# Second halves of six early loads issued from ScalarE's queue

## The chip, the core and the metric

The kernel runs on one core of one Trainium2 chip. A core has five engines that run side by side: TensorE (matmuls, PE in the profile, with its weight loads as PEld), VectorE (DVE), ScalarE (ACT), GpSimd (POOL) and SyncE (SP), which here only issues DMAs. The metric is the device time of one execution in microseconds (us); the less the better.

## The reference

Two layers follow each other, for 8 batches of 576 tokens. The first is a linear attention with 8 heads of 64, normalised per head; the second is a mixture of 4 attention experts, of which each token uses two. In short:

```python
kv  = einsum('bhsd,bhse->bhde', k, v)
out = einsum('bhsd,bhde->bhse', q, kv)
x   = out / sqrt(mean(out * out, -1) + 1e-6) * g_norm        # then heads side by side: [b, 576, 512]
logits = x @ w_gate                                          # top 2 of 4 experts, softmax over the two
for e in range(4):
    a = softmax(causal(x @ wq[e] @ (x @ wk[e]).T / 8))
    y += gate[e] * (a @ (x @ wv[e]) @ wo[e])
```

Inputs are q, k and v of shape (8, 8, 576, 64) and the weights, all float32.

## The kernel before

The work is cut by batch, and within a batch into five blocks of tokens, four of 128 and one of 64. For each batch `kv` (line 405) makes the 64x64 products of k and v for four pairs of heads; k and v come in large loads `lk` and `lv` of the first 512 tokens (line 306) and in two small ones each, `lkr` and `lvr`, of the last 64 tokens (line 322), one for each half of the heads. The product is copied to the tile `kvx` (`kvc`, lines 283 and 285), multiplied with the gate weights (`kgm`, line 425), summed (`kgr`, line 432), and the sums are put beside it (`kgx`). `out` (line 466) then multiplies a block of transposed q with it. For batches 0 and 1 q is transposed by matmuls with an identity (`q`, line 448) from blocks that `lq` loads (line 336), each block by two DMAs, one for each half of the heads; from batch 2 on VectorE transposes it (line 456). Then come the norm, the transposition of the normalised tokens (`x`, line 567), the projections to v (line 626), q and k (line 645) of the experts, attention (lines 672, 686, 706), the output product (line 764) and the stores. The weights of the experts are loaded early into `w_stage` (`lw`, line 378) and scaled by g_norm (`ws`, line 384).

Nothing is scheduled by the compiler: `ORDER` is one long list of tasks written out by hand, and each engine, and each DMA queue, executes its own tasks in that order. `ENGINE` says for copies and elementwise tasks which engine does them, and `SLOTS` which buffer a tile takes. Loads and stores are issued by SyncE, except in batch 0 for the loads of v, which ScalarE issues at the very start (`queue`, line 290). Around the change the list reads, in order (task, batch, part; the engine for those of ScalarE):

```
lvr 0 (ACT), lq 0,4, lv 0,0 (ACT), lk 0,2, lv 0,1 (ACT), lkr 0, lv 0,2 (ACT), lv 0,3 (ACT), lk 0,1, q 0,4, lk 0,3,
gb, qc 0,4 (ACT), lk 0,0, lq 1,2, lq 0,3, kv 0,2, lq 0,0, gr, g8, lvr 1, kv 0,1, wg, kv 0,3, lq 0,2, kv 0,0,
kgm 0,1, kvc 0,1, lq 0,1, kvc 0,0 (ACT), kgm 0,0, kgr, lk 1,1, q 0,3, lq 1,4, kgx, lv 1,0, out 0,4, lkr 1, lk 1,0, lv 1,1, lw v,1 ...
```

In batch 0 a `lk` or `lv` brings two heads (256 KB), later four (512 KB). A half of a q block of 128 tokens is 128 KB, a half of a remainder 64 KB. `ZEROS` puts filler matmuls on zeros ahead of some tasks of the start (line 796).

Of the kernel before, what the change touches and what calls it, by code (L numbers as in the profile page):

```python
# [16 lines left out]
NB, NCH, EP, NF = 5, 4, 2, 4  # L17
# [5 lines left out]


ZEROS = {("q", 0, 4): 8, ("gb",): 2, ("kv", 0, 2): 6, ("kv", 0, 1): 3, ("q", 0, 3): 3}

ORDER = (
    "090E010403080507020u060H0v003F0D0c0A0F0G3C0b0J0I0d0C0a0j0i0B0e0f0k390s0g3H0l0m0h0t381A0n163B1C1B1D0w3718170o19"
# [90 lines left out]
def kernel(  # L119
# [13 lines left out]
    nc = tc.nc  # L133
    P = nc.NUM_PARTITIONS
    B, H, S, Dh = q.shape
# [3 lines left out]
    REM = S - NF * P  # L139
# [72 lines left out]
    kr, vr, kvx, lg8s, vexts, mss, sqs, rstds, roots = [], [], [], [], [], [], [], [], []  # L212
# [77 lines left out]
    def queue(b, second):  # L290
        return nc.scalar if b == 0 and second else nc.sync

    def q_t(b):
        if b in QPE:
            return buf(("q", b), [P, NB, 2, NCH * Dh], FP32, "q_b")
        return buf(("q", b), [P, NCH, S // 32, 32], FP32, "q_b")
# [19 lines left out]
        if (b, p) == (0, NCH - 1):  # L316
            nc.scalar.preload_act_table_set("natural_log_exp_and_others")

    def load_rem(eng, dst, src, b):
        for a in range(2):  # L320
            hs = slice(a * NCH, (a + 1) * NCH)
            eng.dma_start(dst[a * REM : (a + 1) * REM, hs, :], src[b, hs, NF * P : S, :].rearrange("h p d -> p h d"))

    def lkr(b):
        load_rem(nc.sync, kr[b % 2], k, b)

    def lvr(b):
        load_rem(queue(b, True), vr[b % 2], v, b)

    def lq(b, i):  # L330
        eng = nc.sync
        if b in QPE:
            t0, nt = blocks[i]
            n = NCH * nt // P * Dh
            for a in range(2):
                eng.dma_start(
                    q_t(b)[:, i, a, 0:n], q[b, a * NCH : (a + 1) * NCH, t0 : t0 + nt, :].rearrange("h (p j) d -> p h (j d)", p=32)
                )
            return
        r, c0, n = i % 4, i // 4 * 2, 2 * (S // 32)  # L340
        h0 = NCH * (r // 2) + c0
        eng.dma_start(
            q_t(b)[r * 32 : (r + 1) * 32, c0 : c0 + 2].rearrange("p c g d -> p (c g) d"),
            q[b, h0 : h0 + 2, :, (r % 2) * 32 : (r % 2 + 1) * 32].rearrange("h (g t) d -> t (h g) d", t=32),
        )
# [427 lines left out]
    def store(b, qc):  # L773
# [4 lines left out]

    emit = dict(
        lk=lk, lv=lv, lkr=lkr, lvr=lvr, lq=lq, gr=gr, g8=g8, gb=gb, wg=wg, lw=lw, ws=ws, lwo=lwo, wo=wo,  # L780
        kv=kv, kvc=kv_copy, q=q_tr, qc=q_copy, kgm=kvg_mul, kgr=kvg_sum, kgx=kvg_copy,
        out=out_mm, oc=o_copy, sq=square, red=red, ln=ln, rs=rs, na=newton_a, nb=newton_b, nc=newton_c, nd=newton_d, gl=gl, lg=lg, xm=xm, x=x_tr, xc=x_copy,
# [5 lines left out]
    def zero_matmuls(n, count):  # L788
        if n[0] == "kv":
            t, lo = small("kv", n[1]), NCH * Dh  # L790
        elif n[0] in ("q", "x", "v", "y"):
            t, lo = small(*n), 0
        else:
            t, lo = big(*{"qp": ("q",), "kp": ("k",)}.get(n[0], (n[0],)), *n[1:])[:, 0], 0
        for _ in range(count):
            nc.tensor.matmul(
                t[:, lo:512], lhsT=zeros[:, 0:P], rhs=zeros[:, lo:512], start=True, stop=True, skip_group_check=True
            )
# [28 lines left out]
    with tc.manual_schedule():  # L827
        for n in order:
            touched.clear()
            traced = len(nc.cur_bb.bb.instructions)  # L830
            if n in ZEROS:
                zero_matmuls(n, ZEROS[n])
            emit[n[0]](*n[1:])
# [32 lines left out]
```

The softmax here doesn't subtract the row's maximum and nothing guards it: scores larger than these inputs give would overflow.

## Time and profile before

| | before |
|---|---|
| time, median of 3 runs | 226.26 us (225.9 to 227.05) |
| span of the profiled execution | 225.8 us |
| TensorE busy | 211.3 us (94%) |
| VectorE busy | 157.5 us (70%) |
| ScalarE busy | 133.5 us (59%) |
| GpSimd busy | 125.8 us (56%) |
| moved by DMA | 40.29 MB, mean 178 GB/s |
| read from HBM, written to it | 30.42 MB, 9.44 MB |

A share of busy time is a mean over the span. In the first 60 us, where the loads of batches 0 to 3 and all weights arrive, the engines are less busy than later: TensorE works for 8.21 of the first 10 us and 8.41 of the next, and for all of the 20 us from 60 to 80. In the timelines that follow, a row gives the start, the length, the engine, the line, the operation, what it writes and reads, and how many are merged in the row; in square brackets stands the idle time of the engine just before, with what ended it. SPq and ACTq are the instructions by which SyncE and ScalarE issue DMAs; their length is the time of the issuing, not of the transfer.

### The profile page before, as it was taken

What the parts mean: (1) busy time and instruction counts of PE and PEld (TensorE: products, weight loads), DVE (VectorE), ACT (ScalarE), POOL (GpSimd) and SP (SyncE); (2) the same over time, 40 slices, a digit from 0 to 9 for tenths busy, and PEclk for the clock granted to TensorE, in tenths of its full rate; (3) what the DMA queues carried; (4) which work ended last, traced back from release to release, by engine and by line L of the source; (5) the groups of instructions that cost most, each with busy time, mean ns of one, the idle gap of its engine ahead of it and who ended that gap; (6) DMA issues with size and microseconds to landing.
All of it is one profiled execution on the core that took longest, in us unless ns stands there. A gap on an engine that the chain in (4) does not pass through costs nothing. (4 is left out here: it accounts for less than half of the span.)

```text
span 225.8 us, 6620 instructions
## 1 busy us (share of the span) xinstructions
PE 211.3 (94%) x2562; PEld 178.9 (79%) x2562; DVE 157.5 (70%) x366; ACT 133.5 (59%) x265; POOL 125.8 (56%) x278
## 2 busy tenths in 40 slices
PE   7988798988999998999999999999999999999981
PEld 3467797977899798897998699878878899799550
DVE  6275669738475798689797865589996476843570
ACT  0215742876649752759526964866764992664951
POOL 8400775077517693469715970479549869712520
PEclk9999999999699999999999999999999999999998
DMA  4988978998999677999899897998334000040065
GB/s 124 325 233 258 302 181 219 346 231 123 164 321 251 121 176 242 197 167 203 218 248 255 254 237 197 162 221 177 82 99 161 3 0 4 23 186 3 0 215 209
DMA packets 92576, 40.29 MB, mean 178 GB/s; under 512 B 66688, under 2 KB 88192, under 8 KB 92544
## 3 DMA queue, kind: packets, MB, share of 16 engines
q1 hardware_dynamic: 90784, 38.68, 71.2%
q10 hardware_dynamic: 1632, 1.18, 1.9%
q8 instruction: 20, 0.33, 0.7%
q14 instruction: 12, 0.10, 0.2%
q0 software_dynamic: 128, 0.01, 0.0%
HBM read 30.42 MB, written 9.44 MB: 177 GB/s over the span
## 5 line engine op out<-in xcount | busy, mean ns | idle before, releaser
L686 ACT ACTIVATE PT<-p 128x1024 bf16<-128x1024 f32 (+1 forms) x64 | 50.3, 841 | 6.6 <-PE p L672 6.1
L692 POOL TENSOR_SCALAR_AFFINE_SELECT PT<-PT 128x256 bf16<-128x256 bf16 (+1 forms) x80 | 29.1, 382 | 26.7 <-ACT PT L686 25.8
L557 POOL TENSOR_TENSOR x_tok<-o_sb,rstd 128x512 fp32r<-128x512 f32 x40 | 43.1, 1130 | 0.5
L466 PE MATMUL p<-kvx,qT 128*128 128x136 f32 (+1 forms) x320 | 39.1, 285 | 0.7 <-DVE kvx L285 0.7
L466 PEld LDWEIGHTS p<-kvx,qT 128*128 128x128 f32 (+1 forms) x320 | 34.7, 179 | 3.2 <-DVE kvx L285 0.9
L502 DVE TENSOR_REDUCE ms<-sq 128x8 f32<-128x520 f32 (+1 forms) x40 | 27.0, 684 | 7.5 <-POOL sq L498 3.6
L498 POOL TENSOR_TENSOR sq<-o_sb 128x512 f32<-128x512 f32 (+1 forms) x20 | 20.6, 1038 | 12.7 <-DVE ms L502 6.4
L626 PE MATMUL p<-wv_r,xT 128*128 128x256 f32 x160 | 25.9, 298 | 1.4 <-POOL wv_r L384 0.7
L567 PE MATMUL p<-ident_r,x_tok 128*128 128x128 f32 (+1 forms) x160 | 23.4, 279 | 0.7 <-DVE vext L285 0.3
L626 PEld LDWEIGHTS p<-wv_r,xT 128*128 128x128 f32 x160 | 21.5, 195 | 2.7 <-issue 0.8
L567 PEld LDWEIGHTS p<-ident_r,x_tok 128*128 128x128 f32 x160 | 20.6, 191 | 3.8 <-POOL x_tok L557 1.0
L672 PE MATMUL p<-qTp,kT 64*128 64x64 f32 (+4 forms) x192 | 22.2, 346 | 1.3 <-DVE kT L285 0.6
L283 ACT COPY o_sb<-p 128x544 f32<-128x544 f32 (+1 forms) x29 | 15.1, 532 | 13.0 <-PE p L466 12.6
L764 PE MATMUL p<-wo_b,OT 128*128 128x512 bf16 (+1 forms) x96 | 20.4, 348 | 0.7 <-ACT OT L283 0.5
L405 PE MATMUL p<-v_b,k_b 128*64 128x64 f32 x512 | 20.1, 224 | 0.9 <-DMA k_b<-in_k_dram 0.9
L645 PE MATMUL p<-xT,wk_r 128*128 128x288 f32 x128 | 20.8, 305 | 0.0
L405 PEld LDWEIGHTS p<-v_b,k_b 128*64 128x64 f32 x512 | 17.8, 138 | 3.2 <-issue 2.1
L645 PE MATMUL p<-xT,wq_r 128*128 128x288 f32 x128 | 19.8, 300 | 0.0
L672 PEld LDWEIGHTS p<-qTp,kT 64*128 64x128 f32 x192 | 14.4, 188 | 6.4 <-ACT PT L686 1.4
L645 PEld LDWEIGHTS p<-xT,wk_r 128*128 128x128 f32 x128 | 17.6, 188 | 1.5 <-DVE xT L285 0.5
L285 DVE COPY o_sb<-p 128x544 f32<-128x544 f32 (+1 forms) x19 | 12.0, 630 | 9.5 <-PE p L466 4.2
L706 PEld LDWEIGHTS <-PT 128*128 128x128 bf16 x480 | 16.2, 98 | 2.4 <-issue 0.8
(111 smaller groups left out, 348.2 us busy)
## 6 DMA issues: line engine op xcount, KB each, us to landing
out_dram<-y SPq DMA_DIRECT2D x32, 256.0 KB, 2.5
k_b<-in_k_dram SPq DMA_DIRECT2D x14, 512.0 KB, 6.4
v_b<-in_v_dram SPq DMA_DIRECT2D x14, 512.0 KB, 6.0
q_b<-in_q_dram SPq DMA_DIRECT2D x48, 144.0 KB, 4.7
q_b<-in_q_dram SPq DMA_DIRECT2D x16, 128.0 KB, 3.9
k_b<-in_k_dram SPq DMA_DIRECT2D x4, 256.0 KB, 5.4
v_b<-in_v_dram ACTq DMA_DIRECT2D x4, 256.0 KB, 5.2
k_rem<-in_k_dram SPq DMA_DIRECT2D x16, 64.0 KB, 5.1
```

Source lines behind the costliest of these rows:

```text
L405: nc.tensor.matmul(p_kv[hh * Dh : (hh + 1) * Dh, c, :], lhsT=lhs, rhs=rhs, start=(j == 0), stop=(j == NF), skip_group_check=True,)
L466: nc.tensor.matmul(p_o[p0 : p0 + nt, c // 2, c % 2 * 256 : c % 2 * 256 + 2 * GW], lhsT=qTs[b % NQT][:, c * S + i * P : c * S + i * P + nt] ...
L498: nc.gpsimd.tensor_tensor(out=dst, in0=src, in1=src, op=AluOpType.mult)
L502: nc.vector.tensor_reduce(mss[b % 2][:nt, i, :], sqs[(NB * b + i) % 3][:nt], axis=AX_X, op=AluOpType.add)
L557: nc.gpsimd.tensor_tensor(out=buf(("x", b, i), [P, NCH, P], FP32R, "x_tok")[:].rearrange("p c (h r) -> p h r c", h=H), in0=ob[:, i, :, 0:D ...
L567: nc.tensor.matmul(p_t[:, c * P : c * P + nt], lhsT=tiles["x", b, i][:, c, :], rhs=ident_r[:, 0:nt], start=True, stop=True)
L626: nc.tensor.matmul(p_v[:, 0 : E * Hd], lhsT=blocks_of(xTs[b % 2], c)[:, i * P : (i + 1) * P], rhs=w_r["v"][:, c, :, :].rearrange("p e f -> ...
L645: nc.tensor.matmul(p_p[:, s, 0:HALF], lhsT=w_r[nm][:, c, 2 * pr : 2 * pr + 2, :].rearrange("p e f -> p (e f)"), rhs=blocks_of(xTs[b % 2], ...
L672: nc.tensor.matmul(p_s[:, el, o : o + hi - lo], lhsT=kTs[(2 * b + pr) % 3][pp, kb * P : (kb + 1) * P], rhs=tiles["qTp", b, pr][pp, lo:hi], ...
L686: nc.scalar.activation(PT[:, :, d0 : d0 + o], big("sc", b, pr, j)[:, :, 0:o], ACTF.Exp, scale=scale)
L692: nc.gpsimd.affine_select(out=d, in_=d, compare_op=AluOpType.is_ge, fill=0.0, base=0, pattern=[[0, 2], [1, w]], channel_multiplier=-1,)
L764: nc.tensor.matmul(p_y[o * nq : (o + 1) * nq, 0:w], lhsT=lhs, rhs=wo_b[:, pr, o * w : (o + 1) * w], start=(pr == 0), stop=(pr == EP - 1), ...
```

## The change

Six loads of the start, each made of two DMAs for the two halves of the heads, all of them issued by SyncE until now, are divided between two queues: SyncE goes on issuing the first half (a = 0), and ScalarE issues the second (a = 1). They are the q blocks 2 of batch 1 and 3, 0, 2 and 1 of batch 0, and the v remainder of batch 1. What is loaded, where to, and the order of the tasks stay as they were. The purpose is that SyncE, which issues one DMA after the other at the start, has six fewer to issue, so that the ones behind them can leave sooner.

```diff
+SPLIT = {("lq", 1, 2), ("lq", 0, 3), ("lq", 0, 0), ("lvr", 1), ("lq", 0, 2), ("lq", 0, 1)}
...
+    def half_of(task, eng, a):
+        return nc.scalar if a and task in SPLIT else eng
+
-    def load_rem(eng, dst, src, b):
+    def load_rem(task, eng, dst, src, b):
         for a in range(2):
             hs = slice(a * NCH, (a + 1) * NCH)
-            eng.dma_start(dst[a * REM : (a + 1) * REM, hs, :], src[b, hs, NF * P : S, :].rearrange("h p d -> p h d"))
+            half_of(task, eng, a).dma_start(dst[a * REM : (a + 1) * REM, hs, :], src[b, hs, NF * P : S, :].rearrange("h p d -> p h d"))
...
-        load_rem(nc.sync, kr[b % 2], k, b)
+        load_rem(("lkr", b), nc.sync, kr[b % 2], k, b)
...
-        load_rem(queue(b, True), vr[b % 2], v, b)
+        load_rem(("lvr", b), queue(b, True), vr[b % 2], v, b)
...
             for a in range(2):
-                eng.dma_start(
+                half_of(("lq", b, i), eng, a).dma_start(
                     q_t(b)[:, i, a, 0:n], q[b, a * NCH : (a + 1) * NCH, t0 : t0 + nt, :].rearrange("h (p j) d -> p h (j d)", p=32)
                 )
```

## The prediction

> **What bounds the kernel now.** I read the page first, then the waits of each engine, then the timelines of the first 60 us of TensorE, ScalarE and SyncE, and last the table by stretches with its DMA column. The page says which engine the time belongs to:
>
> ```profile
> PE 211.3 (94%) x2562; PEld 178.9 (79%) x2562; DVE 157.5 (70%) x366; ACT 133.5 (59%) x265; POOL 125.8 (56%) x278
> ```
>
> TensorE is busy for 211.3 of 225.8 us, so a change to loads can pay only where a load makes TensorE wait, directly or through another engine. The waits of TensorE, GpSimd and VectorE that end in a load are few:
>
> ```profile
> PE p L405 <- DMA k_b<-in_k_dram: 0.9, 1, 0.9
> PE p L626 <- POOL wv_r L384: 0.7, 1, 0.7
> ...
> POOL wv_r L384 <- DMA w_stage<-in_moe_wv_dram: 1.0, 1, 1.0
> ...
> DVE wk_r L384 <- DMA w_stage<-in_moe_wk_dram: 3.5, 1, 3.5
> ```
>
> The columns are total, number and longest. TensorE waits once, 0.9 us, for a load of k, and once, 0.7 us, for GpSimd's scaling of wv, which itself sat 1.0 us until its weights landed. The timelines say when:
>
> ```profile
> 35.85 1.18 PE L626 MATMUL p<-wv_r,xT 128*128 128x256 f32 x8 [0.67 <-POOL wv_r L384]
> ...
> 47.56 0.72 PE L405 MATMUL p<-v_b,k_b 128*64 128x64 f32 x15 [0.90 <-DMA k_b<-in_k_dram]
> ```
>
> None of these is a load that the change touches: they come 20 and 30 us later in the same queue. What lies between is the issue of SyncE:
>
> ```profile
> 7.71 3.87 SPq L336 DMA_DIRECT2D q_b<-in_q_dram  x6
> 11.62 1.29 SPq L322 DMA_DIRECT2D v_rem<-in_v_dram  x2
> 12.96 2.90 SPq L336 DMA_DIRECT2D q_b<-in_q_dram  x4
> 15.90 0.59 SPq L306 DMA_DIRECT2D k_b<-in_k_dram  x1
> ...
> 20.39 0.51 SPq L306 DMA_DIRECT2D v_b<-in_v_dram  x1
> ```
>
> The twelve issues of the six loads run from 7.71 to 15.86 us, back to back, 0.64 us apart, and the large loads of batch 1 only begin at 15.90. Meanwhile the DMA engines run dry (columns: stretch, length, busy of PE, PEld, DVE, ACT, POOL, clock, DMA share, GB/s):
>
> ```profile
> 10.00:12.00 2.00, 2.00 (x45) 1.69 (x43) 0.83 (x3) 0.00 (x0) 0.00 (x0) 1.00 1.10 349
> 12.00:14.00 2.00, 2.00 (x51) 1.46 (x47) 1.26 (x3) 0.00 (x0) 0.00 (x0) 1.00 1.05 307
> 14.00:16.00 2.00, 1.16 (x17) 0.85 (x16) 1.33 (x5) 1.11 (x3) 0.00 (x0) 1.00 0.56 149
> 16.00:18.00 2.00, 1.25 (x18) 1.01 (x20) 1.75 (x6) 0.59 (x1) 0.00 (x0) 1.00 0.67 162
> ```
>
> 349 GB/s until 12 us, 149 and 162 from 14 to 18, then about 295 again: SyncE's issue is the limit from 14 to 18 us. ScalarE has time in just that place:
>
> ```profile
> 5.60 1.28 ACT L317 ACT_TABLE_LOAD   x1 [5.60 <-DMA v_rem<-in_v_dram]
> 6.90 0.37 ACT L283 COPY qT<-p 128x256 f32<-128x256 f32 x1
> 14.74 0.53 ACT L283 COPY kvx<-p 64x128 f32<-64x128 f32 x2 [7.47 <-DVE kvx L285]
> ```
>
> In program order the six moved issues fall between the copy at 6.90 and the kvx copy at 14.74, a hole of 7.47 us. But that kvx copy is on the start-up chain: it begins 0.1 us after VectorE's copy of the other half ends, VectorE's product with wg waits for it 0.66 us at 15.30, and the first output matmul (17.84) waits for what follows.
>
> One more limit shows in the trace's record of the issues. The loads of SyncE and ScalarE share eight completion semaphores, handed out in turn, so each issue waits for the landing of the load eight before it. At 10.40 SyncE issued a half of q as the load of k landed at 10.38; after 11 us the load eight before had landed up to 1.5 us ahead of the issue, so there the 0.64 us an issue is the limit, not the eight.
>
> **What the Trainium skill says.** "DMA: Bandwidth & Descriptors", section "Issuing engines are not separate DMA queues": initiating DMAs on several engines "will only save the time on the sequencer it takes to initiate the DMA, which is usually small relative to the DMA itself." The trace agrees on the engines being common, but here the time is not small: 0.64 us an issue against 0.37 us that a half of q, 128 KB, takes at 349 GB/s. The same page, "Queues, rings and completion order", says that each DMA engine takes its queue rows round-robin, a packet at a time. So a half on ScalarE's queue no longer stands behind SyncE's k loads; it shares with them. In the trace of before both queues do move data side by side from 5 to 10 us; it does not show how fairly.
>
> **The change, part by part.** *Removed from SyncE:* six issues at 0.64 us, 3.8 us. *Added to ScalarE:* six issues. Its own issues took 0.37 to 0.86 us at the start; I take SyncE's 0.6, 3.7 us in all, inside the hole of 7.47 us. *Added waits:* those on the load eight before, now with ScalarE's copy queued behind them.
>
> Walk through with the landings of before (the two small k loads 7.70 and 8.81; v 8.12, 9.25, 10.58; k 10.38, 11.34, 12.09). Each half goes when its slot is free: q halves on SyncE at 7.7, 8.8, 10.4, on ScalarE at 8.1, 9.3, 10.6. These hardly move; the slots, not the issue, hold them. The v remainder goes at about 11.6 on SyncE and, behind the last k load of batch 0, at about 12.5 on ScalarE; q halves then at 12.5 and 13.7 on SyncE, 13.1 and 13.8 on ScalarE, whose last issue ends at about 14.4. That is 0.3 us before the copy at 14.74: hidden, narrowly.
>
> *The k loads of batch 0:* one or two halves of q (128 KB each) now share the DMA engines with them from about 10 us, when the v loads leave ScalarE's queue. At 349 GB/s that is 0.37 to 0.73 us. The last k load then lands at 12.46 to 12.82 instead of 12.09; its matmuls start at 12.63. The one before lands at up to 11.7; its matmuls start at 12.05, so it costs nothing. TensorE loses between 0 and 0.3 us; I take 0.1.
>
> *What moves:* the first large load of batch 1 goes at about 14.4 instead of 15.90, and those behind it keep that until a slot holds one. The first v load of batch 1, now at 17.77, stands behind a q half whose slot a v remainder holds until about 16.0 (16.18 now), so it goes at about 16.6: 1.2 us earlier. From 18 us on the queue is full of 512 KB loads and the DMA engines are the limit, so the whole stream arrives 1.2 us earlier. I find nothing of the computation in its way until about 50 us: the one long issue at 32.65 (1.37 us) comes with its buffer free (a tile of tokens last read at 29 us) and behind a load of 128-byte pieces.
>
> *What that is worth:* wv for GpSimd lands at 33.5 instead of 34.68, so the scaling starts when GpSimd comes free at 33.73. The 0.67 us wait of TensorE goes, but the output matmul that follows two blocks later needs ScalarE's kvx copy, which ends at 36.58, against its start at 36.95 now. So 0.35 us stays, 0.25 after the 0.1 lost at the start. At 47.56 the k load landed at 47.42; 1.2 us earlier is 46.2, and TensorE would come there at 46.66 - 0.25 = 46.4. So the 0.90 us goes as well: 0.25 + 0.90 = 1.15 us. Then ScalarE takes some back: between the attention matmuls and the kvx copy of batch 2 at 51.19 it has a weight copy that waited 0.77 us for a load landing at 48.47, and three exponentials, 2.1 us, whose start can move by about 0.9 us. VectorE's wk, 50.21, moves by 1.2 us into its own idle time of 3.52 us and frees nothing more. So 0.9 us at 56 us. From there to 210 us TensorE has 1.4 us of waits in all, none for a load, so I carry the 0.9 us to the end: 226.26 - 0.9 = 225.4 us.
>
> **The rivals.** *All of it, and more:* both waits of TensorE go in full and ScalarE follows, 0.67 + 0.90 = 1.57 us, 224.7 us. For it: both waits end in late loads, and ScalarE's own wait of 0.77 us goes too. Against it: the 36.58 of the kvx copy and the exponentials. *Hidden anyway:* the gain of 1.2 us at 18 us is eaten by the eight slots and by the full queue before 34 us. For it: the issues at 26.81 and 28.68 leave as the load eight before lands (26.79, 28.67), and the last 512 KB load of batch 1, landing at 28.67, holds no one up. Then the wait at 47.56 shortens by 0.3 us at most: 226.0 us. *Slower:* ScalarE's last issues run past 14.74, or the shared DMA engines delay the last k load past 12.6. For it: the margin of the first is 0.3 us, and 12.82 is past 12.63. Each microsecond late is a microsecond on the start-up chain, and nothing on it waits for the loads that come earlier. Two slots on ScalarE that land 0.6 us later than I put them make its last issue end at 15.6, 0.9 us late; with 0.2 us for the k load that is +1.1 us, 227.4 us, less what the wait at 47.56 gives back, which ends with the load and not with TensorE. Against it: half of ScalarE's hole is free.
>
> **How the numbers follow.** The forecast gets 0.42, all of it and more 0.25, hidden anyway 0.18, slower 0.15. Half a per cent is 1.13 us, so 225.13 is the edge of faster: the second case lies beyond it, and a third of the first, 0.39 in all; slower, past 227.39, is most of the last case, 0.11; the rest, 0.50, is within half a per cent. The range runs from 224.4, a little beyond the best case, to 227.0, past the hidden case and the milder part of the slow one.
>
> **What would show it.** Right: the six issues on ScalarE between 8 and 14.4 us and its kvx copy still at about 14.7; the first large k load of batch 1 issued near 14.4; over 200 GB/s from 14 to 18 us; the waits of GpSimd for wv and of TensorE for k_b gone or under 0.3 us, and the next matmuls on k of batch 2 near 46.4 instead of 47.56. Wrong: a kvx copy later than 14.8, a first output matmul later than 17.9, k matmuls of batch 0 with an idle time ending in a load, or an unchanged landing at 47.4 in spite of that earlier issue.

## The result, and the profile after

The change made the kernel slower: 232.97 us (median of 6 runs, 231.6 to 235.79) against 226.7 us (median of 6, 225.9 to 227.74). The ratio is 1.0269, 95% interval 1.0202 to 1.0335; it leaves out the run of 235.79 us, which fell in a slower state that the kernel before shows at times as well. The forecast was 225.4 us, a gain of 0.9 us, so the time is about 7.6 us from it, and on the other side of the kernel before.

The page of the changed kernel, to be held against the first one: TensorE is busy as long as before (211.2 against 211.3 us), the span is 4.1 us longer.

```profile
span 229.9 us, 6604 instructions
...
PE 211.2 (92%) x2550; PEld 179.2 (78%) x2562; DVE 156.8 (68%) x366; ACT 133.2 (58%) x265; POOL 125.5 (55%) x278
```

The waits of TensorE, then of VectorE and ScalarE, in the changed kernel (total, number, longest). Line numbers are now up to 5 higher: 453 is the transposition of q, 430 the product with the gate weights, 284 ScalarE's copies.

```profile
PE p L453 <- DMA q_b<-in_q_dram: 5.8, 1, 5.8
...
DVE kvg L430 <- ACT kvx L284: 12.0, 3, 7.3
...
ACT kvx L284 <- DMA q_b<-in_q_dram: 14.5, 1, 14.5
```

TensorE has a wait that the kernel before did not have: 5.8 us for a load of q. VectorE waits 7.3 us, where it waited 0.66, for ScalarE's kvx copy, and that copy, which had followed VectorE's at once, ends an idle time of 14.5 us that the profile puts down to a load of q. The timeline of ScalarE shows what stood in front of it:

```profile
6.57 0.37 ACT L284 COPY qT<-p 128x256 f32<-128x256 f32 x1
14.25 3.42 ACTq L341 DMA_DIRECT2D q_b<-in_q_dram  x3
17.70 0.63 ACTq L327 DMA_DIRECT2D v_rem<-in_v_dram  x1
19.41 1.93 ACTq L341 DMA_DIRECT2D q_b<-in_q_dram  x2
21.44 0.53 ACT L284 COPY kvx<-p 64x128 f32<-64x128 f32 x2 [14.49 <-DMA q_b<-in_q_dram]
```

The six issues do not run from 8 to 14.4 us as forecast, but from 14.25 to 21.34. ScalarE was free at 6.94 and did nothing for 7.3 us. SyncE, in the same run, had gone far ahead:

```profile
7.46 1.93 SPq L341 DMA_DIRECT2D q_b<-in_q_dram  x3
9.63 0.62 SPq L327 DMA_DIRECT2D v_rem<-in_v_dram  x1
10.42 1.19 SPq L341 DMA_DIRECT2D q_b<-in_q_dram  x2
11.65 0.59 SPq L307 DMA_DIRECT2D k_b<-in_k_dram  x1
12.28 1.18 SPq L341 DMA_DIRECT2D q_b<-in_q_dram  x2
13.51 1.22 SPq L307 DMA_DIRECT2D v_b<-in_v_dram  x1
14.77 1.29 SPq L327 DMA_DIRECT2D k_rem<-in_k_dram  x2
```

The trace records with each issue which of the eight completion semaphores the load will raise when it has landed. A slot is one use of one of these semaphores, and the records settle the order of the slots. Between the first half of the first divided load (7.46, the 15th DMA in the rotation of eight) and its second half (14.25, the 27th) stand eleven issues of SyncE: five other first halves, one large k load, a q block of batch 1 in two, one large v load and both k remainders. Each issue waits for the landing of the load eight before it in that rotation. For ScalarE's first issue this is SyncE's q half issued at 10.42, which used the same semaphore (number 103 in the record). Its time to landing is 3.8 us, so it landed at 14.2 (14.23 in the record):

```profile
q_b<-in_q_dram SPq DMA_DIRECT2D x1, 128.0 KB, 3.8
```

ScalarE issued at 14.25. Its fifth waited for the large v load issued at 13.51, landed at 19.38, and went at 19.41. So large loads of batch 1, whose first matmul came at 28.92 in the kernel before, were in front of the halves that the start needs, and the kvx copy stood behind all six issues.

TensorE in the same stretch, in the timeline of the kernel before and then of the changed one:

```profile
14.07 1.09 PE L448 MATMUL p<-ident_f,q_b 128*64 128x128 f32 x16
16.05 1.09 PE L448 MATMUL p<-ident_f,q_b 128*64 128x128 f32 x16 [0.89 <-DVE kvg L425]
17.84 2.73 PE L466 MATMUL p<-kvx,qT 128*64 128x136 f32 x24 [0.70 <-DVE kvx L285]
```

```profile
14.08 0.43 PE L453 MATMUL p<-ident_f,q_b 128*64 128x128 f32 x2
20.35 1.97 PE L453 MATMUL p<-ident_f,q_b 128*64 128x128 f32 x14 [5.83 <-DMA q_b<-in_q_dram]
22.75 1.75 PE L453 MATMUL p<-ident_f,q_b 128*64 128x128 f32 x16 [0.43 <-DVE kvg L430]
24.55 2.73 PE L471 MATMUL p<-kvx,qT 128*64 128x136 f32 x24
```

Two matmuls on the first half of q block 3, then 5.83 us of idleness until the second half landed at 20.30. The first output matmul comes at 24.55 instead of 17.84. It needs VectorE's sums as well, which follow the kvx copy:

```profile
22.00 0.69 DVE L430 TENSOR_TENSOR kvg<-p,wg_t 128x512 f32<-128x512 f32 x1 [7.34 <-ACT kvx L284]
22.61 1.27 DVE L437 TENSOR_REDUCE kvxg<-kvg 128x8 f32<-128x512 f32 x2
23.80 0.69 DVE L286 COPY kvx<-kvxg 64x8 f32<-64x8 f32 x4
```

These end at 24.49, and the last transpositions of q end at about the same time (24.50), so two late chains meet there. How the loss runs on, by the starts of single tasks in the two timelines:

| starts at, us | before | after | later by |
|---|---|---|---|
| ScalarE's first kvx copy | 14.74 | 21.44 | 6.70 |
| first output matmul | 17.84 | 24.55 | 6.71 |
| first matmul on k of batch 1 | 28.92 | 35.63 | 6.71 |
| first matmul with wv | 35.85 | 41.85 | 6.00 |
| first matmul on k of batch 2 | 47.56 | 53.26 | 5.70 |
| first matmul on k of batch 3 | 77.58 | 81.72 | 4.14 |
| end of the span | 225.8 | 229.9 | 4.1 |

6.7 us are lost at the start. Two of the old waits for loads (0.67 and 0.90 us) are gone, because the loads had 6.7 us more time; that gives back 1.0 us. The next 1.6 us are the clock's, not the change's: stretches of half speed fall in different places in the two profiles. In the tables by stretches (stretch, length, busy of the five engines, clock, DMA, GB/s) the first row is the kernel before and the next two, in the second fence, the changed one:

```profile
57.00:61.00 4.00, 4.00 (x39) 3.30 (x39) 2.01 (x6) 2.92 (x6) 2.56 (x9) 0.57 1.05 143
```

```profile
57.00:61.00 4.00, 3.51 (x30) 3.31 (x31) 3.38 (x5) 2.29 (x7) 4.00 (x7) 1.00 0.57 102
...
17.00:24.20 7.20, 3.42 (x28) 3.02 (x30) 2.17 (x6) 1.11 (x3) 0.00 (x0) 0.53 1.08 306
```

Before, TensorE was busy in all of the slow stretch; after, it stood still in half of it. From the k matmuls of batch 2 to those of batch 3 it takes 30.02 us before and 28.46 after, where no slow stretch falls. The runs below agree: 28.42 in e1, which has none there either, 29.96 in f4 with one of 3.4 us and 31.56 in e2 with one of 6.8 us. The two profiles are thus 4.1 us apart. The medians are 6.3 us apart; what makes up the rest no trace shows, but two of the six executions of the changed kernel (234.88 and 235.79 us) had a lower granted clock, 0.964 against 0.981 to 0.985 in the others.

### The profile page after: what moved, and what is told of

The parts are those of the page before. It is cut to its first block, busy times and chain, and to the rows that moved or that the text cites. A ratio compares the mean times of both kernels' runs of the same rounds, so it can differ in the third digit from the quotient of the medians.

```text
span 229.9 us, 6604 instructions
## 1 busy us (share of the span) xinstructions
PE 211.2 (92%) x2550; PEld 179.2 (78%) x2562; DVE 156.8 (68%) x366; ACT 133.2 (58%) x265; POOL 125.5 (55%) x278
## 5 line engine op out<-in xcount | busy, mean ns | idle before, releaser
L562 POOL TENSOR_TENSOR x_tok<-o_sb,rstd 128x512 fp32r<-128x512 f32 x40 | 42.6, 1120 | 0.5
L631 PE MATMUL p<-wv_r,xT 128*128 128x256 f32 x160 | 25.1, 291 | 0.7 <-ACT xT L284 0.7
L631 PEld LDWEIGHTS p<-wv_r,xT 128*128 128x128 f32 x160 | 20.8, 189 | 1.9 <-ACT xT L284 0.8
L650 PE MATMUL p<-xT,wq_r 128*128 128x288 f32 x128 | 19.8, 300 | 0.0
L769 PE MATMUL p<-wo_b,OT 128*128 128x512 bf16 (+1 forms) x85 | 18.2, 343 | 1.7 <-issue 0.5
L677 PEld LDWEIGHTS p<-qTp,kT 64*128 64x128 f32 x192 | 14.2, 185 | 6.3 <-ACT PT L691 1.5
L453 PE MATMUL p<-ident_f,q_b 128*64 128x128 f32 x144 | 11.9, 312 | 7.5 <-DMA q_b<-in_q_dram 5.8
L430 DVE TENSOR_TENSOR kvg<-p,wg_t 128x1024 f32<-128x1024 f32 (+1 forms) x9 | 9.9, 1105 | 12.8 <-ACT kvx L284 12.0
```

Of the source, the lines that this page charges most:

```text
L562: nc.gpsimd.tensor_tensor(out=buf(("x", b, i), [P, NCH, P], FP32R, "x_tok")[:].rearrange("p c (h r) -> p h r c", h=H), in0=ob[:, i, :, 0:D ...
L631: nc.tensor.matmul(p_v[:, 0 : E * Hd], lhsT=blocks_of(xTs[b % 2], c)[:, i * P : (i + 1) * P], rhs=w_r["v"][:, c, :, :].rearrange("p e f -> ...
L650: nc.tensor.matmul(p_p[:, s, 0:HALF], lhsT=w_r[nm][:, c, 2 * pr : 2 * pr + 2, :].rearrange("p e f -> p (e f)"), rhs=blocks_of(xTs[b % 2], ...
L677: nc.tensor.matmul(p_s[:, el, o : o + hi - lo], lhsT=kTs[(2 * b + pr) % 3][pp, kb * P : (kb + 1) * P], rhs=tiles["qTp", b, pr][pp, lo:hi], ...
L769: nc.tensor.matmul(p_y[o * nq : (o + 1) * nq, 0:w], lhsT=lhs, rhs=wo_b[:, pr, o * w : (o + 1) * w], start=(pr == 0), stop=(pr == EP - 1), ...
```

## The experiments

Theory *slots*: ScalarE's issues were late because their completion slots were numbered behind later loads of SyncE. Rival *queue*: loads on ScalarE's queue are slow, or two queues share the DMA engines badly. A second question: is it the copy blocked behind the issues, or the q data that came late?

**Alternating slots (e1).** In the changed kernel ScalarE's queue has a q copy, which waits for TensorE, ahead of the six issues. Given to VectorE, it leaves nothing that waits for TensorE ahead of them, and in this program's record of the semaphores first and second halves take the slots in turn. Nothing else is different.

```diff
     order, engine = unpack(B)
+    engine["qc", 0, 4] = "V"
```

> The change as it stands, and one copy more: the q copy of block 4 (0.37 us), which stands on ScalarE ahead of the six moved issues, is given to VectorE, idle at that time. The six halves then take completion slots alternately with SyncE's. Theory 'slots' (ScalarE's issues came late because their slots were handed out behind ten later loads of SyncE): the six issues leave ScalarE between 8 and 14.5 us, its kvx copy begins at 14.7 to 15.1, the first output matmul at 17.8 to 18.2, the matmuls on k of batch 2 near 46.5, and the time is 225 to 226.5 us, ratio to before 0.993 to 1.001. Rival 'queue' (loads on ScalarE's queue are slow by themselves, or two queues share the DMA engines badly): the halves still land after 19 us, the kvx copy is past 19 us and the time stays over 230 us.

Measured: 225.69 us, ratio to before 0.9953 (0.9924 to 0.9982). ScalarE's and SyncE's timelines, one fence each:

```profile
8.21 2.86 ACTq L342 DMA_DIRECT2D q_b<-in_q_dram  x3
12.03 0.63 ACTq L328 DMA_DIRECT2D v_rem<-in_v_dram  x1
12.78 1.30 ACTq L342 DMA_DIRECT2D q_b<-in_q_dram  x2
14.73 0.53 ACT L285 COPY kvx<-p 64x128 f32<-64x128 f32 x2 [8.04 <-DMA v_rem<-in_v_dram]
```

```profile
12.40 1.28 SPq L342 DMA_DIRECT2D q_b<-in_q_dram  x2
13.96 1.01 SPq L308 DMA_DIRECT2D k_b<-in_k_dram  x1
...
16.65 0.59 SPq L308 DMA_DIRECT2D v_b<-in_v_dram  x1
```

The six issues end at 14.08, the kvx copy begins at 14.73, the first output matmul at 17.83. The halves of q land between 12.76 and 17.54 us. Two queues and the same loads, and no loss is left: the queue is not slow, and the order of the slots was the cause, unless the moved copy mends it by itself, which e2 tests. From 14 to 18 us the DMA engines now move 267 GB/s, where they moved 155 before (the tables by stretches of this run, then of the kernel before):

```profile
14.00:18.00 4.00, 2.41 (x35) 1.87 (x36) 3.07 (x10) 1.69 (x4) 0.00 (x0) 1.00 0.96 267
```

```profile
14.00:18.00 4.00, 2.41 (x35) 1.86 (x36) 3.08 (x10) 1.69 (x4) 0.00 (x0) 1.00 0.61 155
```

**The copy alone (e2).** No load is divided, as in the kernel before, and that q copy is on VectorE. The edit is shown against the changed kernel; with an empty `SPLIT` all issues go to the engines of before.

```diff
-SPLIT = {("lq", 1, 2), ("lq", 0, 3), ("lq", 0, 0), ("lvr", 1), ("lq", 0, 2), ("lq", 0, 1)}
+SPLIT = set()
...
+    engine["qc", 0, 4] = "V"
```

> No half is moved (as before), and the same q copy of block 4 is given to VectorE. This tells what the copy alone does. Both theories: nothing; kvx copy on ScalarE at 14.7, ratio to before 0.996 to 1.004.

Measured: 225.6 us, ratio 0.9967 (0.9942 to 0.9992); the kvx copy on ScalarE at 14.85. In the kernel before, which has no late issues, the copy brings at most a few tenths of a per cent, so by itself it is not worth the 6 us that go in e1. But the time was as good as e1's here, so what the division brings was open, and both were measured twice more (f2 and f3, g1 and g2).

**One half only (e3), and with the kvx copy moved (e4).** Only the second half of q block 2 of batch 1, used at 26.7 us, goes to ScalarE; in e4 the kvx copy of the first half of batch 0 goes to VectorE besides (the last line, in e4 alone).

```diff
-SPLIT = {("lq", 1, 2), ("lq", 0, 3), ("lq", 0, 0), ("lvr", 1), ("lq", 0, 2), ("lq", 0, 1)}
+SPLIT = {("lq", 1, 2)}
...
+    engine["kvc", 0, 0] = "V"
```

> Only the second half of q block 2 of batch 1 is moved to ScalarE; its matmuls come at 26.7 us, so late data cannot hurt. Theory 'blocked copy' (what costs is that the kvx copy stands behind an issue that waits for its slot): the half's slot is that of the load eight before in the rotation, the second v remainder, landing near 16 us; the issue ends near 16.6, the kvx copy begins at 16.6 to 17.0 instead of 14.7, the first output matmul near 19.8, time 228 to 229.5 us. Rival 'late data' (what costs is that the transposes of q lack their second halves): kvx copy and output matmul as before, time 226 to 227.5 us.

> As the run with one half moved, and the kvx copy of the first half of batch 0 is given from ScalarE to VectorE, so that nothing on the start-up chain stands behind the issue. Theory 'blocked copy': the first output matmul is back at 17.6 to 18.0 us and the time at 226 to 227.3 us. Rival 'late data' or a slow queue: no difference from the run with one half.

Measured in e3, the timeline of ScalarE:

```profile
15.47 0.58 ACTq L341 DMA_DIRECT2D q_b<-in_q_dram  x1
16.16 0.53 ACT L284 COPY kvx<-p 64x128 f32<-64x128 f32 x2 [8.69 <-DMA v_rem<-in_v_dram]
```

One issue on ScalarE, waiting for a v remainder, delays the copy to 16.16 and the first output matmul to 19.26, 1.42 us later than before; 0.2 us of it was there already at VectorE's first kvx copy (14.29 against 14.06). The expectation was 19.8, half a microsecond too much, because the v remainder landed at 15.45 and not near 16. In e4 the first output matmul is at 17.80, with the same issue at 15.40. So a copy blocked behind one issue costs by itself, even if the data of that load are not needed for 10 us. The times are of one execution each, 227.06 and 225.21 us, and both lie below what was expected (228 to 229.5 and 226 to 227.3). Executions of the kernel before, measured beside them, run from 224.97 to 231.16 us, so these two times decide nothing; the starts in the traces do.

**All six late, kvx copy moved (f1).** The changed kernel with its slots as they are, and that kvx copy on VectorE.

```diff
     order, engine = unpack(B)
+    engine["kvc", 0, 0] = "V"
```

> The change with its slots as they are (all six second halves late on ScalarE), and the kvx copy of the first half of batch 0 given from ScalarE to VectorE. It splits the loss at the start into its two parts. If the blocked copy is the whole of it, the first output matmul is back near 18 us. If the late halves of q bind as well, TensorE stands at the transposes until about 20.3 (block 3) and 22.7 us (block 0), as in the run of the change, and the first output matmul comes at 23.5 to 24.2 us instead of 24.55: then 5.7 to 6.4 of the 6.7 us are due to late data alone, and the two parts do not add but lie side by side.

Measured: 233.9 us, one run. The timelines of VectorE and of TensorE:

```profile
14.40 1.18 DVE L287 COPY kvx<-p 64x128 f32<-64x128 f32 x4
...
17.41 0.69 DVE L287 COPY kvx<-kvxg 64x8 f32<-64x8 f32 x4
```

```profile
20.86 1.97 PE L454 MATMUL p<-ident_f,q_b 128*64 128x128 f32 x16 [6.02 <-DMA q_b<-in_q_dram]
23.11 1.75 PE L454 MATMUL p<-ident_f,q_b 128*64 128x128 f32 x13 [0.28 <-DMA q_b<-in_q_dram]
24.45 0.43 PE L472 MATMUL p<-kvx,qT 128*64 128x136 f32 x1
```

VectorE has all of kvx ready at 18.1 us, and the first output matmul still comes at 24.45 (24.2 was the most expected). That is 6.6 us later than before; 0.3 us of it was there already at VectorE's first kvx copy (14.40 against 14.06). So with the late halves of q alone 6.3 of the 6.7 us stay. An estimated 0.7 us of them is the clock's: it was at half speed here, and from the start of the transpositions of block 0 (23.11) to the output matmul it took 1.34 us, which would halve. With e3 and e4: both parts are real, they lie side by side, and taking the blocked copy away helps almost nothing while the late halves stand. The opposite, halves in time and the copy still late, was not run; in the changed kernel VectorE's chain behind the copy ends at 24.49, so there too the output matmul could not have come before that.

**Alternating slots and the copy alone, again (f2, f3, g1, g2), and with the kvx copy on VectorE (f4).** The kernels of e1 and e2; f4 is e1 with the line of f1 added.

> The run with alternating slots again, beside the copy alone, to see what the division itself is worth. Theory 'the loads come earlier and something waits for them': ratio to the copy alone 0.995 or less, ratio to before 0.990 to 0.996. Rival 'hidden': the same as the copy alone within 0.2 per cent.

> The copy alone again, as the base for the run with alternating slots: 225.3 to 226.3 us, ratio to before 0.994 to 0.999. TensorE's wait for k of batch 2 at 47 us (0.9 us in the trace of before) is there or not according to when the load lands, 46.5 to 47.5 us.

> Alternating slots, and the kvx copy of the first half of batch 0 on VectorE, so that no copy on the start-up chain stands behind an issue. With alternating slots the issues end 0.6 us before that copy is due, so it should change nothing: within 0.2 per cent of the run with alternating slots. If it is faster by more, the issues still held up ScalarE.

> The copy alone a third time (0.9967 and 1.0033 to before in the two earlier comparisons), now measured ahead of the run with alternating slots. If the copy alone brings nothing: ratio to before 0.997 to 1.003.

> Alternating slots a third time (0.9953 and 0.9965 to before). If the earlier loads are worth something by themselves: ratio to before 0.994 to 0.998 and below that of the copy alone by 0.2 per cent or more. If not: the two agree within 0.2 per cent.

| ratio to before (interval) | first | second | third |
|---|---|---|---|
| alternating slots (e1, f2, g2) | 0.9953 (0.9924 to 0.9982) | 0.9965 (0.9939 to 0.9991) | 0.9970 (0.9945 to 0.9995) |
| copy alone (e2, f3, g1) | 0.9967 (0.9942 to 0.9992) | 1.0033 (1.0006 to 1.0060) | 0.9993 (0.9965 to 1.0021) |
| alternating, kvx on VectorE (f4) | 0.9967 (0.9942 to 0.9993) | | |

With alternating slots the kernel is 0.3 to 0.5% faster than before in all three comparisons, 225.5 to 225.7 us. The copy alone is a little faster, a little slower and the same; its second time, 227.34 us, lies outside the 225.3 to 226.3 that was expected. By the ratios the division, with its slots in turn, is 0.1, 0.7 and 0.2% faster than the copy alone: always on the same side, but the first is less than the 0.2% that the later runs took as the least that counts, and half of the second comes from the long time of the copy alone there. How much the division brings by itself stays open. f4 differs from f2 by nothing: the issues no longer hold up ScalarE. The version of e1 is a little faster than the kernel before and, by the medians, about 3% faster than the changed one.

## Why the prediction was wrong

The step that failed is this one: "Each half goes when its slot is free: q halves on SyncE at 7.7, 8.8, 10.4, on ScalarE at 8.1, 9.3, 10.6." The eight shared slots were seen in the trace of before and used in every step, but their order was taken for granted: first half, second half, as the code's loop emits them. In the changed program the semaphores are handed out in another order, and ScalarE's first half waits for a load that SyncE issued three microseconds after its partner. Everything after that step was worked out for issues at the wrong time.

The rivals saw the place but not the size. *Slower* had the kvx copy behind the issues, put at 0.9 us late where it was 6.7, with a chance of 0.15; its two slots were thought to land 0.6 us late. The late q data were not considered at all: the walk through named the landing of k loads only, and f1 shows that with the q halves alone late 6.3 us are lost. A small misreading changes nothing: the load eight before had landed up to 1.8 us ahead of SyncE's issue after 11 us (the issue at 15.90, the landing at 14.06), not 1.5.

Three of the signs named for being right came true in the slower kernel: the DMA engines moved 302 GB/s from 14 to 18 us, the waits for wv and for k of batch 2 were gone, and the first large k load of batch 1 went at 11.65. They show that loads moved ahead, not that the right ones did; the signs on ScalarE's issues, on its kvx copy and on the first output matmul are those that told the two apart.

The remaining steps can be tested in e1, where the halves do alternate, and there these come out as forecast or nearly so:

| step | forecast | e1 |
|---|---|---|
| ScalarE's issues | 8.1 to 14.4 us | 8.21 to 14.08 |
| kvx copy | about 14.7 | 14.73 |
| first large k load of batch 1 issued | 14.4 | 13.96 |
| first large v load of batch 1 issued | 16.6 | 16.65 |
| output matmul held by ScalarE's kvx copy of batch 1 | 36.6 | 36.61 |
| first matmul on k of batch 2 | 46.4 | 46.58 |
| time | 225.4 us | 225.69, 225.52, 225.57 |

TensorE's waits for wv and for k of batch 2 are gone in e1. The 0.1 us put down to the k loads of batch 0, for sharing the DMA engines with halves of q, is not seen: the last one landed at 12.01, before at 12.09.

That the time fits is in part luck. The stream of loads was to arrive 1.2 us earlier; in e1 the weights wv landed at 31.26, 3.4 us earlier than before, and the last load of k of batch 2 at 43.81, 3.6 us earlier, which is more than TensorE could use. And most of the gain up to 47 us came without the division too: in the three traces of the copy alone wv landed at 33.00 to 33.26, the k load at 45.38 to 46.80, and TensorE began the k matmuls of batch 2 at 46.70 to 46.93 (47.56 before; 46.58 to 47.03 in the three traces of e1, f2 and g2). The prediction took its two waits from the one trace of the kernel before, of an execution of 227.51 us where the median is 226.7; whether other executions have these waits is not known. The "hidden" rival had the gain eaten before 34 us: that is not what e1, f2 and g2 show, where wv landed at 31.26 to 31.63, though in f4 it landed at 33.00. Its outcome, next to no gain from the division, is not excluded.

Why the numbers of the slots came out so was not tried by itself. What the runs show is that taking one copy that waits for TensorE out of ScalarE's queue, ahead of the issues, changes them from "eleven of SyncE first" to "in turn"; taking out the kvx copy, which stands behind the issues, leaves them as they were (f1).

## What to carry to other kernels

Before loads are spread over a second queue, find out what an issue waits for besides its data: where a few completion slots are shared by two queues, as the eight here, an issue can wait for a load of the other queue, and the order of the slots is part of the change, to be read from the new program and not from the loop that emits it. An issue that waits blocks everything behind it on its engine (one held the kvx copy back by 1.4 us in e3, six by 6.7 us in the changed kernel), so a queue with a critical copy behind it should be given only issues whose slots are free. Where a load and a copy are both late, freeing one can show nothing (f1); free each in turn, and both, before calling either harmless.

## What the runs showed of the hardware that was not expected

TensorE's clock drops to half speed for single stretches of about 3.4, 6.8 or 10.2 us, and their place varies: at 57.2 us (3.4 us) in the profile of before, at 17.3 us (6.8 us) in that of after, at 16.6 us (10.2 us) and 64.4 us (3.4 us) in f1, and in e1 only at 222.6 us; one begins within 3.5 us of the end of the span in every profile. It varies between executions of one program too: the copy alone had a stretch at 56.2 us in e2 and none there in f3 and g1. A stretch that falls on idle time costs little, so a difference between two profiles can be off by 1.6 us, as here. The early ones came in the three runs where TensorE's start was held up (after, e3 at 19.7 us, f1), and in none of the other nine profiles. All six executions of the changed kernel had a granted clock of 0.964 to 0.985, the twenty of e1 0.989 to 1.0. That idleness brings the early stretches fits this, but was not tested.

The copy alone, one and the same program, gave 0.9967, 1.0033 and 0.9993, the first two outside each other's intervals. In the one trace of the second comparison, f3, TensorE had two waits for loads of k, 1.7 us in all, that the traces of the other two lack:

```profile
PE p L411 <- DMA k_b<-in_k_dram: 1.7, 2, 0.9
```

These waits would account for most of the difference, but a comparison of some twenty executions has only one trace, so this is not shown. A single comparison of 0.3% says little here.
